# Another table of order and engines for the first two batches of an attention and feed-forward kernel

## The chip, the cores and the metric

The kernel runs on one core of a Trainium2 chip. The metric is device time in microseconds (us) of one launch; the kernel before takes 1108.86 us, the median of three runs (1108.12 to 1110.11). Five engines work side by side, each through its own queue in order: PE (TensorE, matmuls), DVE (VectorE), ACT (ScalarE), POOL (GpSimd) and SP (SyncE, which here only issues DMA transfers). They meet through semaphores.

## The reference

The reference is attention with a thresholded softmax over 8 batches of 8 heads, 576 positions of 64, followed by a feed-forward layer over the 4608 rows that come out of it:

```
scores = scale * q @ k.T
thresh = max(scores) - tau
scores = where(scores >= thresh, scores, -1e9)
attn   = exp(scores - max(scores)); attn /= sum(attn) + 1e-9
x      = (attn @ v), heads side by side            # 4608 x 512
h      = x @ w_in                                   # 512 x 2048
g      = h if h >= 1, 0 if h <= -1, else (h+1)^2/4
out    = g @ w_out                                  # 2048 x 512
```

## The kernel before

All matmuls but those of batch 0's scores run on f16 pairs: a value is split into a high half and a low rest, and each product is three matmuls (high by high, high by low, low by high). The weights arrive as 64-bit numbers, 16 blocks of 128x512 of `w_in` ("i") and 16 of `w_out` ("o"). Each goes through two steps before the feed-forward can use it. The first rebuilds a 32-bit number from the two words (`fix` L845, `low` L855, `b2` L864, `b3` L872); the letter in `SIGN` says how: "A" has ACT do both `fix` and `low`, "N" gives `low` to POOL, "D" gives `fix` to POOL and adds a second DVE instruction (`b3`). The second scales it and splits it into halves (L920 to L958); the letter in `CONV` says how: "A" and "G" are a scaling and a high half on ACT or on POOL and the rest on POOL (L933), "D" is the high half on POOL (L936) and the rest on DVE (L939), "P" and "Q" have PE form the rest and ACT (L949) or DVE (L947) copy it out. ACT's or POOL's results of the first step often need a PSUM bank `ph`, of which there are three.

Scores are computed in tiles of 128 rows by 576 columns, two tiles to a "visit" (`PAIR`: "J" runs the two together, "S" one after the other). A tile goes through a negated minimum on DVE (L1127), a threshold on DVE or ACT (`THR`: L1134 or L1132), the exponential on ACT (L1137), mask and sum on DVE (L1151), normalisation on POOL (L1169, the default) or on ACT (L1172, "N" in `TILE`), the high half on ACT (L1177), the rest on POOL (L1180), a transposing DMA (L1213), and the product with v on PE (L1299). Batch 0 is tiles 0 to 35. The feed-forward goes by groups of 256 rows; its matmuls all stand on line 466, its activation on L1376 to L1393.

The order of the instructions on every engine is not found by dependencies at run time: `Plan.op` numbers some 5000 steps, `ORDER` lists these numbers, and `Plan.order` (L329) walks the list, gives each step a time from its cost and its buffers, and the program is written out in order of these times. Buffers of a pool (PSUM banks `ph` and `s`, SBUF tiles) go to the step that takes them next in the list. Where PE would stand idle within the first 120 us of these times, `gaps` and `keep_warm` (L1451 to L1471) write small matmuls on constants into a free PSUM bank (L1454), which compute nothing that is used: 397 of them.

Of the kernel before, what the change touches and what calls it, by code (L numbers as in the profile page):

```python
# [26 lines left out]
CONV = {"i": "AGAGDAGGPAGAADDP", "o": "PDDAADMDAAPGAGAD"}  # L27

SIGN = {"i": "NNNAAANANANAANNA", "o": "AAAANANAAANANNNA"}
THR = "VVAVAVVVVVVVVVAVAAVVAAAAVVVVVAAVVVVAAVAAVAVVVAAVVVVVVAVVVVVVVVVVVVVVVVVVVVVVVVVVVVVVVVVVVVVVVVVVVVVVVVVVVVVVVVVVVVVVVVVVVVVVVVVVVVVVVVVVVVVVVVVVVVVVVVVVVVVVVVVVVVVVVVVVVVVVVVVVVVVVVVVVVVVVVVVVVVVVVVVVVVVVVVVVVVVVVVVVVVVVVVVVVVVVVVVVVVVVVVVVVVVVVVVVVVVVVVVVVVVVVVVVVVVVVVVVVVVVVVVVVVVVVVVV"  # L30
# [338 lines left out]
def attn_ffn_kernel(ctx: ExitStack, tc: tile.TileContext, qT, kT, vT, tau, w_in, w_out, out):  # L369
# [444 lines left out]
    def add_w(w):  # L814
# [96 lines left out]
        for u in range(NU):  # L911
# [48 lines left out]
            seen, done = [], []  # L960
            for how in plan.ways(("parts " + w, u), CONV[w][u], "PQAGDM"):
                if how in "AG":
# [548 lines left out]
```

## Time and profile before

| | before |
|---|---|
| median of three runs | 1108.86 us |
| the profiled execution | 1107.48 us |
| its span, first to last instruction | 1105.6 us |
| PE busy | 1080.7 us (98%) |
| DVE busy | 910.5 us (82%) |
| ACT busy | 876.5 us (79%) |
| POOL busy | 750.9 us (68%) |
| the L1454 matmuls' share of PE busy | 30.17 us |

The profile comes from one execution. Its own time is 1.38 us under the median of the runs, and 1.88 us of it lie outside the span. A busy share over the whole span says little here, since the first 170 us, where weights are converted beside attention, have other limits than the rest. So the rows below are read stretch by stretch. "Idle before <- X" in a row is idle time of the engine just before the instruction, and X is what released it.

### The profile page before, as it was taken

What the parts mean: (1) busy time and instruction counts of PE and PEld (TensorE: products, weight loads), DVE (VectorE), ACT (ScalarE), POOL (GpSimd) and SP (SyncE); (2) the same over time, 40 slices, a digit from 0 to 9 for tenths busy, and PEclk for the clock granted to TensorE, in tenths of its full rate; (3) what the DMA queues carried; (4) which work ended last, traced back from release to release, by engine and by line L of the source; (5) the groups of instructions that cost most, each with busy time, mean ns of one, the idle gap of its engine ahead of it and who ended that gap; (6) DMA issues with size and microseconds to landing.
All of it is one profiled execution on the core that took longest, in us unless ns stands there. A gap on an engine that the chain in (4) does not pass through costs nothing.

```text
span 1105.6 us, 36892 instructions
## 1 busy us (share of the span) xinstructions
PE 1080.7 (98%) x14677; PEld 800.8 (72%) x14677; DVE 910.5 (82%) x2664; ACT 876.5 (79%) x1682; POOL 750.9 (68%) x870
## 2 busy tenths in 40 slices
PE   8799989999999999999999999999999999999998
PEld 7578658777777777776777677677777677767774
DVE  4899988999889898889899898888888899877222
ACT  5899899898788898887788888778788886776433
POOL 4889997676668886797669786576667885565000
PEclk9699999999999999999999999999999999999999
DMA  9896798786877776798787777758667677558000
GB/s 337 294 272 129 144 205 160 120 147 120 171 135 147 160 137 135 132 156 148 126 148 149 128 151 139 128 114 165 148 114 119 120 123 141 95 97 137 12 20 20
DMA packets 420669, 155.90 MB, mean 141 GB/s; under 512 B 399504, under 2 KB 399504, under 8 KB 420496
## 3 DMA queue, kind: packets, MB, share of 16 engines
q1 hardware_dynamic: 420416, 153.41, 71.2%
q8 instruction: 115, 1.88, 0.7%
q14 instruction: 58, 0.48, 0.2%
q10 hardware_dynamic: 80, 0.13, 0.0%
HBM read 45.09 MB, written 9.44 MB: 49 GB/s over the span
## 4 chain that ended last, share of the span: by engine, by line
PE 80%; DVE 7%; ACT 5%; POOL 3%; issue 2%; DMA 2%; SPq 0%; ACTq 0%; DVEq 0%; POOLq 0%
PE ph L466 30%; PE acc L466 30%; PE s L1073 9%; PE ph L1299 9%; DVE s L1127 2%; DVE e L1151 2%; POOL hl L1180 1%; PE ph L1454 1%; DMA eT<-hl 1%; ACT e L1137 1%; ACT hl L1177 1%; POOL e L1169 1%; DMA x<-in_moe_w_out_dram 1%; DMA qq<-in_q_dram 0%; DVE sm L1134 0%
## 5 line engine op out<-in xcount | busy, mean ns | idle before, releaser
L466 PEld LDWEIGHTS <-WI 128*64 128x64 f16 (+1 forms) x7446 | 407.3, 108 | 53.3 <-issue 16.6
L1180 POOL TENSOR_TENSOR hl<-e,hl 128x576 f16<-128x576 f32 x267 | 347.8, 1311 | 118.0 <-ACT hl L1177 110.5
L466 PE MATMUL ph<-x,WI 128*64 128x256 f16 (+1 forms) x6912 | 400.3, 264 | 0.9 <-DVE x L1311 0.9
L1169 POOL TENSOR_SCALAR e<-e,sm 128x576 f32<-128x576 f32 x253 | 199.3, 792 | 111.9 <-DVE sm L1161 82.8
L1151 DVE SCALAR_TENSOR_TENSOR e<-s,sm,e 128x578 f32<-128x578 f32 x286 | 229.9, 813 | 21.8 <-ACT e L1137 16.4
L1137 ACT ACTIVATE e<-s,sm 128x576 f32<-128x576 f32 x288 | 209.0, 740 | 39.4 <-DVE s L1127 33.1
L1127 DVE TENSOR_SCALAR_CACHE_REDUCE s<-s,pc 128x576 f32<-128x576 f32 x252 | 203.6, 820 | 37.4 <-PE s L1073 36.0
L1177 ACT ACTIVATE hl<-e 128x576 f16<-128x576 f32 x267 | 178.6, 681 | 43.5 <-POOL e L1169 42.2
L466 PE MATMUL acc<-WO,ga 128*64 128x512 f16 (+1 forms) x1590 | 203.8, 380 | 0.2 <-ACT ob L1438 0.2
L1073 PE MATMUL s<-kk,qq 64*128 64x288 f16 (+3 forms) x1840 | 152.0, 299 | 9.1 <-DVE e L1151 8.1
L466 PEld LDWEIGHTS <-ga 128*64 128x64 f16 (+1 forms) x1590 | 91.9, 109 | 81.2 <-issue 9.8
L1383 DVE SCALAR_TENSOR_TENSOR ph<-ph,fcs,asq 128x512 f32<-128x512 f32 (+1 forms) x160 | 111.7, 700 | 45.2 <-ACT asq L1379 44.0
L1376 ACT ACTIVATE asq<-ph,fcs 128x512 f32<-128x512 f32 (+1 forms) x160 | 116.1, 735 | 37.9 <-PE ph L466 37.2
L1299 PE MATMUL ph<-eT,vst 128*64 128x320 f16 (+2 forms) x1928 | 123.8, 279 | 4.5 <-DMA eT<-hl 3.7
L1299 PEld LDWEIGHTS <-vst 128*64 128x64 f16 x1928 | 102.3, 110 | 23.1 <-issue 11.5
L1073 PEld LDWEIGHTS <-qq 64*128 64x128 f16 (+1 forms) x1680 | 66.3, 96 | 49.8 <-issue 37.4
L1388 ACT ACTIVATE ga<-ph,fcs 128x256 f16<-128x256 f32 (+1 forms) x160 | 70.3, 451 | 30.3 <-DVE ph L1383 23.7
L1379 ACT ACTIVATE asq<-asq 128x512 f32<-128x512 f32 x144 | 90.3, 629 | 3.2
L1393 DVE SCALAR_TENSOR_TENSOR ga<-ph,fcs,ga 128x256 f16<-128x256 f32 (+1 forms) x160 | 70.6, 449 | 24.2 <-ACT gb L1388 9.6
L466 PE MATMUL acc<-WO,gb 128*64 128x512 f16 (+1 forms) x582 | 75.0, 379 | 0.0
L466 PE MATMUL acc<-WO,WI 128*64 128x512 f16 (+1 forms) x534 | 68.3, 380 | 0.0
L466 PE MATMUL acc<-WO 128*64 128x512 f16 (+1 forms) x510 | 64.6, 380 | 0.0
(185 smaller groups left out, 1181.1 us busy)
## 6 DMA issues: line engine op xcount, KB each, us to landing
raw<-in_v_dram SPq DMA_DIRECT2D x32, 288.0 KB, 3.6
WO<-in_moe_w_in_dram SPq DMA_DIRECT2D x16, 512.0 KB, 7.3
out_dram<-ob SPq DMA_DIRECT2D x32, 256.0 KB, 2.8
raw<-in_q_dram SPq DMA_DIRECT2D x28, 288.0 KB, 3.4
raw<-in_k_dram SPq DMA_DIRECT2D x28, 288.0 KB, 3.2
x<-in_moe_w_out_dram SPq DMA_DIRECT2D x10, 512.0 KB, 5.9
eT<-hl SPq DMA_TRANSPOSE x288, 3.5
WO<-in_moe_w_out_dram SPq DMA_DIRECT2D x4, 512.0 KB, 5.0
```

Source lines behind the costliest of these rows:

```text
L466: T.matmul(out[x], lhsT[:, x], rhs, **flags)
L1073: T.matmul(ap(sb, s_ps)[r, f, :SH], q, k, start=ql == kl == 0, stop=exact or ql == 1)
L1127: V.tensor_scalar(sv(), sv(), c, None, ALU.mult, ALU.min, accum_out=t[:, 0:1])
L1137: A.activation(ev(), sv(), AF.Exp, bias=ap(m, sm)[:, 0:1], scale=-1.0)
L1151: V.scalar_tensor_tensor(ev(SH + 1), sv(SH + 1), t[:, 2:3], ev(SH + 1), ALU.is_le, ALU.mult, accum_out=t[:, 3:4])
L1169: G.tensor_scalar(ev(), ev(), ap(m, sm)[:, 5:6], ESC, ALU.mult, ALU.mult)
L1177: A.activation(part2(0), ev(), AF.Copy)
L1180: G.tensor_tensor(part2(w), ev(), part2(0), ALU.subtract)
L1299: T.matmul(o[hd * D : (hd + 1) * D, :n], vt[:, k, hd * D : (hd + 1) * D], t[:, kb, (hd ^ p % 2) * n : ((hd ^ p % 2) + 1) * n], start=m == ...
L1376: A.activation(tv()[:, :, c], hv()[:, :, c], AF.Relu, bias=fcs[:, b, 2, q : q + 1], scale=fcs[:, b, 3, q : q + 1])
L1379: A.activation(ap(tb, asq), ap(tb, asq), AF.Square)
L1383: V.scalar_tensor_tensor(hv()[:, :, c], hv()[:, :, c], fcs[:, b, 0, q : q + 1], tv()[:, :, c], ALU.max, ALU.min)
```

## The change

Only tables change: `CONV`, `SIGN`, `THR`, `PAIR`, `TILE` and `ORDER`. No function is touched.

```diff
-CONV = {"i": "AGAGDAGGPAGAADDP", "o": "PDDAADMDAAPGAGAD"}
+CONV = {"i": "AGAGGAGGPAGAADDP", "o": "PDDAADMGAAQGAGAD"}
-SIGN = {"i": "NNNAAANANANAANNA", "o": "AAAANANAAANANNNA"}
+SIGN = {"i": "NNNAADANAAANANAA", "o": "AAAANANAAANANNNN"}
-TILE = {3: "S", 5: "N", 7: "N", 8: "N", 18: "V", 20: "N", 25: "V", 26: "N", 27: "N", 28: "N", 29: "V", 32: "N", 35: "N", 40: "N", 44: "N", 54: "N", 55: "V", 58: "N", 59: "N", 69: "V",
+TILE = {3: "S", 5: "N", 8: "N", 18: "V", 20: "N", 22: "N", 25: "V", 26: "N", 27: "N", 29: "V", 30: "N", 32: "N", 55: "V", 69: "V",
...
 ORDER = [
-    605, 606, 607, 608, 12, 13, 14, 15, 0, 1, 590, 595, 596, 580, 585, 16, 17, 592, 600, 18, 597, 610, 5, 615, 19, 20, 21, 22, 591, 2, 598, 635, 581,
...
```

In words: block 4 of `w_in` and block 7 of `w_out` go from "D" to "G", block 10 of `w_out` from "P" to "Q". In `SIGN`, block 5 of `w_in` becomes "D", blocks 6, 8, 10 and 14 become "A", blocks 7 and 11 become "N", and block 15 of `w_out` becomes "N". In batch 0 the tiles 7, 28 and 35 leave the list of those that ACT normalises and 22 and 30 join it; in batch 1 the tiles 40, 44, 54, 58 and 59 leave it. Of the thresholds seven more go to ACT, four of them ahead of the first feed-forward product of the second group of rows. Of the visits 3, 5, 15 and 16 are joined, and 6, 7, 12 and 18 are parted. The keep-warm matmuls of L1454 fall from 397 to 314.

SP's queue near the start: `raw` are blocks of v, `WO` from `in_moe_w_in_dram` are staged blocks of w_in, `kk0` and `qq0` are k and q of the first heads. Before, from the tenth transfer on:

```order
L571 DMA kk0_76<-in_k_dram 128x576 [waits DMAHW3_49]
L839 DMA WO_68<-in_moe_w_in_dram 128x1024 [waits DMAHW4_49]
L513 DMA tcs_138<-in_tau_dram 128x1 [waits DMAHW5_49]
L839 DMA WO_68<-in_moe_w_in_dram 128x1024 [waits DMAHW6_49,DVE_49]
L571 DMA qq0_80<-in_q_dram 128x576 [waits DMAHW7_49]
L839 DMA WO_68<-in_moe_w_in_dram 128x1024 [waits DMAHW0_49,DVE_49,Activation_49]
```

And now, from the tenth on:

```order
L839 DMA WO_68<-in_moe_w_in_dram 128x1024 [waits DMAHW3_49]
L839 DMA WO_68<-in_moe_w_in_dram 128x1024 [waits DMAHW4_49]
L571 DMA kk0_76<-in_k_dram 128x576 [waits DMAHW5_49]
L571 DMA qq0_80<-in_q_dram 128x576 [waits DMAHW6_49]
L839 DMA WO_68<-in_moe_w_in_dram 128x1024 [waits DMAHW7_49,DVE_49]
L839 DMA WO_68<-in_moe_w_in_dram 128x1024 [waits DMAHW0_49,DVE_49]
```

The load of q is issued ahead of the block of w_in that waits for a DVE instruction, and no longer behind it.

ACT's queue at the exponentials of tiles 3 and 2 (into the buffers `e2` and `e3`; L862 is `low` of a weight block into a PSUM bank `ph`). Before:

```order
L1177 ACTIVATE hl0_93<-e1_90 128x576 [waits Pool_49]
L1137 ACTIVATE e2_91<-s1_62,sm2_124 128x2x288 [waits DVE_49]
L862 ACTIVATE ph1_64<-x4_107 128x512 [waits DMAHW4_49,PE_49]
L1137 ACTIVATE e3_92<-s0_61,sm3_125 128x2x288 [waits DVE_49]
L1132 ACTIVATE sm3_125<-sm3_125,tcs_138 128x1
L853 ACTIVATE x2_105<-x2_105 128x512 [waits DMAHW0_49]
```

And now:

```order
L1177 ACTIVATE hl0_93<-e1_90 128x576 [waits Pool_49]
L862 ACTIVATE ph0_63<-x4_107 128x512 [waits DMAHW5_49,DVE_49]
L1137 ACTIVATE e2_91<-s1_62,sm2_124 128x2x288 [waits DVE_49]
L1132 ACTIVATE sm3_125<-sm3_125,tcs_138 128x1 [waits DVE_49]
L1137 ACTIVATE e3_92<-s0_61,sm3_125 128x2x288
L862 ACTIVATE ph2_65<-x2_105 128x512 [waits DMAHW6_49,DVE_49]
```

The `low` that stood between the two exponentials and waited for PE stands ahead of both, in another bank, and waits for DVE and its load instead.

POOL's queue some rows on, at block 4 of w_in (`hl` are tiles' rests). Before, L936 is the high half of block 4, the L924 ahead of it scales block 6, the L930 and last L933 split block 6, and the first L933 is the rest of block 5:

```order
L924 TENSOR_SCALAR WI_67<-WI_67,wsc_i_141 128x512
L936 TENSOR_SCALAR WI_67<-WI_67,wsc_i_141 128x512
L933 TENSOR_TENSOR WI_67<-WI_67 128x512
L1180 TENSOR_TENSOR hl0_93<-e1_90,hl0_93 128x576
L1169 TENSOR_SCALAR e0_89<-e0_89,sm0_122 128x2x288
L860 TENSOR_SCALAR WO_68<-WO_68 128x512
L930 TENSOR_SCALAR WI_67<-WI_67 128x512
L933 TENSOR_TENSOR WI_67<-WI_67 128x512
```

And now, where the first L930 and L933 are those of block 4 (whose scaling stands a few rows ahead), and the second pair splits block 6:

```order
L860 TENSOR_SCALAR WO_68<-WO_68 128x512
L930 TENSOR_SCALAR WI_67<-WI_67 128x512
L933 TENSOR_TENSOR WI_67<-WI_67 128x512
L930 TENSOR_SCALAR WI_67<-WI_67 128x512
L933 TENSOR_TENSOR WI_67<-WI_67 128x512
L1180 TENSOR_TENSOR hl2_95<-e3_92,hl2_95 128x576
```

POOL has three instructions for block 4 where it had one.

## Rows read from the trace of the kernel before

**Rows 1.** Timeline of PE, the first 256-column product: start, us, engine, line.

```profile
168.91 5.41 PE L466 MATMUL ph<-x,WI 128*64 128x256 f16 x96
```

**Rows 2.** Windows: us; busy of PE, PEld, DVE, ACT, POOL; clock; DMA share; GB/s.

```profile
0.00:22.60 22.60, 19.81 (x232) 17.82 (x232) 7.54 (x24) 10.48 (x20) 8.27 (x46) 1.00 0.92 335
22.60:89.00 66.40, 56.18 (x632) 43.66 (x631) 60.55 (x178) 59.10 (x111) 56.83 (x70) 0.87 0.99 277
89.00:159.00 70.00, 66.45 (x791) 47.56 (x792) 66.49 (x193) 64.79 (x129) 67.17 (x74) 1.00 0.80 152
169.00:1000.00 831.00, 829.02 (x11743) 615.74 (x11739) 730.30 (x2154) 685.62 (x1309) 598.71 (x658) 1.00 0.75 136
```

**Rows 3.** The first three windows again, keep-warm matmuls of L1454 alone: PE busy.

```profile
0.00:22.60 22.60, 11.78 (x148) 1.00 0.92 335
22.60:89.00 66.40, 14.36 (x189) 0.87 0.99 277
...
sum 159.00, PE 30.17; mean PE 10.06
```

**Rows 4.** The chain of waits from 28 to 48 us: start, us, what.

```profile
31.78 3.92 PE ph L1454 x39
...
35.73 0.63 ACT ph L862
...
37.24 0.84 DVE e L1151 x2
...
42.48 1.27 POOL hl L1180
```

**Rows 5.** Timeline of ACT, one wait: start, us, engine, line [idle before <-releaser].

```profile
35.73 0.63 ACT L862 ACTIVATE ph<-x 128x512 uint32<-128x512 uint32 x1 [1.73 <-PE ph L1454]
```

**Rows 6.** The chain of waits from 88 to 105 us.

```profile
92.78 1.61 PE acc L1454 x27
94.40 1.18 PE s L1073 x7
```

**Rows 7.** Groups by line and form, 0 to 169 us: count | busy us, mean ns.

```profile
L1169 POOL TENSOR_SCALAR e<-e,sm 128x576 f32<-128x576 f32 x26 | 20.9, 807 | 3.4 <-DVE sm L1161 2.0 <-ACT WO L922 0.8 <-DVE sm L1203 0.4
L933 POOL TENSOR_TENSOR WI<-WI 128x512 f16<-128x512 f32 x11 | 12.7, 1161 | 0.3
L1172 ACT ACTIVATE e<-e,sm 128x576 f32<-128x576 f32 x9 | 7.0, 779 | 0.0
L870 DVE SCALAR_TENSOR_TENSOR WI<-WO,ph 128x512 uint32<-128x512 uint32 x8 | 5.3, 675 | 7.7 <-ACT ph L862 7.7
L1134 DVE TENSOR_SCALAR sm<-sm,tcs 128x1 f32<-128x1 f32 x25 | 5.3, 213 | 0.8
L1132 ACT ACTIVATE sm<-sm,tcs 128x1 f32<-128x1 f32 x15 | 4.2, 286 | 0.0
L924 POOL TENSOR_SCALAR WI<-WI,wsc_i 128x512 f32<-128x512 f32 x5 | 3.5, 695 | 5.2 <-DVE tcs L507 5.1
L939 DVE SCALAR_TENSOR_TENSOR WI<-WI,wsc_i 128x512 f16<-128x512 f32 x3 | 3.4, 1138 | 0.0
L930 POOL TENSOR_SCALAR WI<-WI 128x512 f16<-128x512 f32 x5 | 3.1, 617 | 0.7 <-PE ph L942 0.4
```

**Rows 8.** Timeline of DVE at the first attention tile.

```profile
24.96 0.68 DVE L868 SCALAR_TENSOR_TENSOR WI<-ph,WO 128x512 uint32<-128x512 uint32 x1
25.56 0.81 DVE L1127 TENSOR_SCALAR_CACHE_REDUCE s<-s,tcs 128x576 f32<-128x576 f32 x1
```

**Rows 9.** Who POOL waited for, 22.6 to 89 us: us, times, longest.

```profile
POOL hl L1180 <- ACT hl L1177: 4.8, 3, 2.3
```

**Rows 10.** One window of PE's low clock (columns of rows 2).

```profile
38.50:52.00 13.50, 11.07 (x55) 7.87 (x54) 11.12 (x31) 11.64 (x21) 10.76 (x14) 0.51 0.81 226
```

**Rows 11.** Timeline of PE, two like visits at different clocks.

```profile
24.24 2.09 PE L1073 MATMUL s<-kk,qq 64*128 64x288 f32 x8
...
46.47 3.98 PE L1073 MATMUL s<-kk,qq 64*128 64x288 f32 x8 [2.43 <-DVE e L1151]
```

More of the change, by code (lines that the diff above doesn't have):

```diff
@@ L25 @@
 XJ, XS = 1.2, 1.0
-CONV = {"i": "AGAGDAGGPAGAADDP", "o": "PDDAADMDAAPGAGAD"}
-SIGN = {"i": "NNNAAANANANAANNA", "o": "AAAANANAAANANNNA"}
-THR = "VVAVAVVVVVVVVVAVAAVVAAAAVVVVVAAVVVVAAVAAVAVVVAAVVVVVVAVVVVVVVVVVVVVVVVVVVVVVVVVVVVVVVVVVVVVVVVVVVVVVVVVVVVVVVVVVVVVVVVVVVVVVVVVVVVVVVVVVVVVVVVVVVVVVVVVVVVVVVVVVVVVVVVVVVVVVVVVVVVVVVVVVVVVVVVVVVVVVVVVVVVVVVVVVVVVVVVVVVVVVVVVVVVVVVVVVVVVVVVVVVVVVVVVVVVVVVVVVVVVVVVVVVVVVVVVVVVVVVVVVVVVVVVVV"
-PAIR = "SJSSSSJJJSSSJJJSSJJJJJJJJJJJJJJSJJJJJJJJJJJJJJJJJJJJJJJJJJJJJJJJJJJJJJJJJJJJJJJJJJJJJJJJJJJJJJJJJJJJJJJJJJJJJJJJJJJJJJJJJJJJJJJJJJJJJJJJJJJJJJJJ"
+CONV = {"i": "AGAGGAGGPAGAADDP", "o": "PDDAADMGAAQGAGAD"}
+SIGN = {"i": "NNNAADANAAANANAA", "o": "AAAANANAAANANNNN"}
+THR = "VVAVVVVVVVAAVVAAAAAAAAAAVAVVVVAVVVAAVVAAVVAAVVVVAAAAVVAVVVVVVVVVVVVVVVVVVVVVVVVVVVVVVVVVVVVVVVVVVVVVVVVVVVVVVVVVVVVVVVVVVVVVVVVVVVVVVVVVVVVVVVVVVVVVVVVVVVVVVVVVVVVVVVVVVVVVVVVVVVVVVVVVVVVVVVVVVVVVVVVVVVVVVVVVVVVVVVVVVVVVVVVVVVVVVVVVVVVVVVVVVVVVVVVVVVVVVVVVVVVVVVVVVVVVVVVVVVVVVVVVVVVVVVVV"
+PAIR = "SJSJSJSSJSSSSJJJJJSJJJJJJJJJJJJSJJJJJJJJJJJJJJJJJJJJJJJJJJJJJJJJJJJJJJJJJJJJJJJJJJJJJJJJJJJJJJJJJJJJJJJJJJJJJJJJJJJJJJJJJJJJJJJJJJJJJJJJJJJJJJJJ"
 QHOW = "DDPDPPDPPPDDPPPPPPPPPPPPPDDPPPPP"
@@ L248 @@
 NPLAIN = 4
-TILE = {3: "S", 5: "N", 7: "N", 8: "N", 18: "V", 20: "N", 25: "V", 26: "N", 27: "N", 28: "N", 29: "V", 32: "N", 35: "N", 40: "N", 44: "N", 54: "N", 55: "V", 58: "N", 59: "N", 69: "V", 71: "V", 94: "V", 114: "V", 117: "V", 150: "V", 152: "V", 173: "V", 181: "V", 186: "V", 200: "V", 214: "S", 222: "V", 257: "V", 262: "V", 287: "V"}
+TILE = {3: "S", 5: "N", 8: "N", 18: "V", 20: "N", 22: "N", 25: "V", 26: "N", 27: "N", 29: "V", 30: "N", 32: "N", 55: "V", 69: "V", 71: "V", 94: "V", 114: "V", 117: "V", 150: "V", 152: "V", 173: "V", 181: "V", 186: "V", 200: "V", 214: "S", 222: "V", 257: "V", 262: "V", 287: "V"}
 FSCALE = "GGGGGGGG"
```

401 rows, old and new, of the table ORDER are left out of this document.

## The prediction

> **What bounds the kernel now.** I read the page's busy shares first: PE is far ahead of the others (98%, DVE 82%). So I asked next where PE is not busy or busy for nothing, with a table of windows and the same table for the keep-warm matmuls alone. From 169 to 1000 us PE is busy 829.02 of 831 us [rows 2]: there it is the bound, and an engine that gets more or less to do changes nothing while it stays under its neighbours (POOL 72%, DVE 88%). Before that, PE loses time: to 22.6 us 2.8 idle and 11.78 keep-warm, from 22.6 to 89 us 10.2 idle and 14.36 keep-warm, from 89 to 159 us 3.55 idle and the remaining 4.03 keep-warm [rows 2, 3]. The first product over 256 columns, the second group's, starts at 168.91 [rows 1] and marks the change. What the tables can win or lose is won or lost in this lead. Its limit is the three elementwise engines together: from 22.6 to 89 us DVE, ACT and POOL are busy 91%, 89% and 86%, from 89 to 159 us 95%, 93% and 96% [rows 2]. None has much room; they pass the work round and wait a little for each other. The first 22.6 us are loading: DMA busy 0.92 at 335 GB/s [rows 2]. The change leaves PE's useful work as it is, so the time follows from when the lead ends.
>
> **The change part by part.** I make the sum against the profiled execution's own 1107.48 us (span 1105.6 and 1.88 outside it), and move it to the median of the runs, 1108.86, by the 1.38 us between them.
>
> *Term a, ACT's wait for a keep-warm block.* In the chain of waits from 28 to 48 us stands a block of 39 keep-warm matmuls, 3.92 us; when it ends, ACT starts a weight block's `low` in the same PSUM bank, behind it in ACT's queue comes an exponential, and DVE masks with that at 37.24 [rows 4]. ACT had been idle 1.73 us [rows 5]. In the new order that `low` is ahead of both exponentials and waits for no PE work, and the block of 39 is gone. What is late next: DVE, whose list just before the mask loses the rest of block 4 (1.138 us, [rows 7]), then PE's next scores, which waited for that mask. I take 1.73 as won. The ends are 0, if the POOL work that follows in the same chain up to 43.75 [rows 4] hides it, and 3.92, the whole block.
>
> *Term b, a shorter keep-warm block at 92.78.* There the chain goes from 27 keep-warm matmuls, 1.61 us, straight to scores [rows 6]. The block has 13 now: 14 x 1.61/27 = 0.83 us won. It is 0 if the scores' operands or their bank come only then, as the planned gap suggests, and can be no more than 1.61.
>
> *Term c, work that changes engines in the lead.* Counted ahead of the first feed-forward product of the second group of rows (168.91, [rows 1]). Two blocks go from "D" to "G": each gives POOL a scaling, a high half and a rest, 0.695 + 0.617 + 1.161, for one scaled high half, which I price like the scaling (0.695): 1.778 more, and takes 1.138 from DVE [rows 7]; two make 3.56 and -2.28. Tiles 7, 28 and 35 come to POOL and 22 and 30 go to ACT: one more normalisation on POOL, 0.807, one less on ACT, 0.779 [rows 7] (the scalar-sized divisors left out). Four more thresholds go to ACT: -4 x 0.213 = -0.85 on DVE, +4 x 0.286 = 1.14 on ACT [rows 7]. `SIGN` evens out on ACT and POOL by counts (one `low` for one `fix` on each) and gives DVE one `b3`; its nearest row is L870, 0.675 [rows 7]. Block 10 of w_out moves one copy out of PSUM from ACT to DVE; DVE has no row for it, and the rows of its shape lie between 0.617 and 1.161; I take L870, which also reads PSUM, for both engines [rows 7]. Sums: POOL +4.37, DVE -1.78, ACT -0.31, together +2.28. The three are about equally full, so if the order keeps them so, the lead grows by a third of it, 0.76 us. The ends are -1.78 (DVE alone is the bound) and +4.37 (POOL alone is). The five tiles of batch 1 that leave ACT come after 169 us: POOL gets 5 x 0.807 there, hidden under PE's 99.8%.
> VectorE's rest of a block has a mean of 1.138 us [rows 7]. The Trainium skill (SBUF — State Buffer, "SBUF: two separate sides") says that VectorE and GpSimd hold a shared port pair exclusively for a whole instruction, and that the other fully blocks; by that rule part of this price is waiting for GpSimd, which is given more to do here, so that DVE would get back less than the row says. By it the gain of 2.28 on DVE would be an upper bound, and the term somewhat above 0.76; no row here says how much.
>
> *Term d, the first tile.* The load of the first q stood behind a load of w_in that waits for DVE; now it goes ahead, with one block of w_in (512 KB, at 335 GB/s [rows 2] 1.56 us) less before it. DVE is in the way, though: its list up to the first tile's minimum at 25.56 is busy, and of it only the 0.68 us at 24.96 [rows 8] are moved behind the minimum. I take these 0.68 as won; the ends are 0 and 1.56. DVE does that work later all the same; the gain is that ACT's and POOL's first attention work comes sooner.
>
> *Elsewhere.* Of eight visits four are joined and four parted, all on PE; its 10.2 us of idle time from 22.6 to 89 us and 3.55 behind that [rows 2] hide what does not cancel. Were that cover gone, one visit more or less would be up to 2.09 us [rows 11].
>
> Sum: -1.73 - 0.83 + 0.76 - 0.68 = -2.48 us. From 1107.48 that is 1105.0, and from the median 1108.86 it is 1106.4.
>
> **The rivals.** *Fewer idle PE slots, all of it kept.* The order has 83 keep-warm matmuls fewer. In this trace 397 took 30.17 us of PE [rows 3], 0.076 each; 83 are 6.3 us. If useful work moves up into all of that, the time is 1108.86 - 6.3 = 1102.6. For it: from 169 us on every us that PE starts earlier is kept, since it idles 2 in 831. Against it: the blocks only fill gaps, and what PE waits for in the gaps are three engines at 86 to 96%.
>
> *POOL hides the gain.* After the mask at 37.24 the chain goes through POOL [rows 4]; if POOL, with block 4 added at just this place, is what comes last anyway, term a is 0 and the sum -0.75: 1108.1.
>
> *POOL becomes the bound of the lead, and the kernel is slower.* From 89 to 159 us POOL is busy 67.17 of 70 us, more than DVE (66.49) and ACT (64.79) [rows 2], and the last rests of batch 0 stand at the end of its list. The change puts 4.37 us on it. Before 89 us it has 9.6 us of idle time, but half of that (4.8 us, three waits for ACT's high half [rows 9]) comes from a tile's way from POOL to ACT and back, and work added ahead of such a trip moves the trip rather than fills it. Then the end of batch 0 comes 4.37 us later, the gains of a, b and d lie on engines that wait for POOL, and the time is 1113.2. The point from which it decides is the first stretch in which POOL's list has no wait, here 89 us. Against it: POOL would start earlier with tiles 0 to 3 (terms a and d).
>
> *PE's clock.* From 38.5 to 52 us PE runs at the lower of its two levels (0.51 granted, [rows 10]). A visit took 2.09 us at 2.4 GHz and 3.98 at 1.2 [rows 11]. What PE did before the fall was the block of 39 and a pause for the mask; the new order has no such block there. If one more visit falls into the low stretch, 1.89 us come back, and the sum is -0.59: 1108.3. The Trainium skill (TensorE: Matmul & The Clock Gate, "What's actually happening") has it that the default state is throttled and activity releases it; by that rule taking keep-warm work away speaks for this rival. The trace agrees in so far as the low window is the one with 2.4 us of PE idle among 13.5 [rows 10].
>
> **How the numbers follow.** I give the forecast 0.42, with its own range from 1104.0 to 1108.4 (each of a, b and d between half and one and a half of its value, c between 0 and 1.6); all of the keep-warm time kept 0.13, the gain hidden by POOL 0.17, POOL as bound 0.20, the clock 0.08. A measurement can tell about 0.2%, 2.2 us, from no change: faster means under 1106.6, slower over 1111.1. Faster: a little over half of the forecast, all of the first rival, a little of the second: 0.41. Slower: nearly all of POOL as bound and small parts of the rest, 0.25. Within: 0.34. The range for 8 in 10 goes from 1102.5, where the first rival ends, to 1112.0, within the POOL case, whose full 4.37 needs all its gaps to stay.
>
> **What would show it.** Term a: no wait of ACT for a keep-warm matmul between 30 and 45 us, and the mask of tile 2 about 2 us before 37.24. Term b: scores right behind 13 keep-warm matmuls with no idle PE. Term d: the first L1127 at about 24.9. Term c: in a window like 89 to 159 us, DVE under POOL by more than now. All together: the first 256-column product of L466, at 168.91 now, 2 to 3 us sooner, and behind it PE at 99.8% as before. I am wrong if that product starts sooner and the end does not, or if POOL shows no wait from some point before 89 us on and that product is late: then POOL was the bound. A low clock well beyond 52 us would speak for the clock.

## The result: 11 us faster, and the profile after

| | median of the runs, us | its runs | ratio to before |
|---|---|---|---|
| before | 1109.03 | 1108.12 to 1110.11 (4) | |
| after | 1098.07 | 1096.96 to 1099.07 (4) | 0.990, 95% interval 0.9887 to 0.9912 |

The forecast was 1106.4, with 1102.5 as the lower end: the direction was right, the size was off by more than a factor of four (2.5 us against 11.0). The profiled execution of after took 1099.07 us (span 1097.3), the slowest of its four runs, and that of before 1107.48, under the fastest of its own, so the two traces differ by only 8.4 us. The other 2.6 of the 11 us are the distance of these two executions from their medians, and no trace shows where they lie.

The 256-column product, in PE's timeline of after (columns as in [rows 1]):

```profile
161.60 0.61 PE L466 MATMUL ph<-x,WI 128*64 128x256 f16 x8
```

It starts 7.31 us earlier than 168.91 [rows 1]. The windows of after (columns as in [rows 2]):

```profile
0.00:22.60 22.60, 19.80 (x237) 17.66 (x238) 9.69 (x29) 10.52 (x20) 9.77 (x49) 1.00 0.93 341
22.60:89.00 66.40, 55.19 (x654) 42.57 (x655) 60.98 (x187) 63.52 (x123) 63.56 (x78) 0.90 1.06 288
89.00:159.00 70.00, 66.45 (x730) 43.79 (x730) 65.84 (x189) 63.88 (x130) 66.96 (x75) 1.00 0.89 161
162.00:1000.00 838.00, 835.77 (x11845) 619.35 (x11843) 734.53 (x2163) 687.62 (x1316) 610.86 (x672) 1.00 0.75 137
```

Behind the product PE is busy 99.7%, 99.8% before [rows 2]; from the product to the end of the span it is 935.7 us now and 936.7 before. So of the 8.3 us by which the traced spans differ, 7.31 lie in the lead. From 22.6 to 89 us ACT is busy 63.52 us (59.10 before) and POOL 63.56 (56.83), in the same 66.4 us. The keep-warm matmuls of L1454 in the first three windows of after (busy of PE and PEld; clock; DMA share; GB/s):

```profile
0.00:22.60 22.60, 12.20 (x158) 10.83 (x158) 1.00 0.93 341
22.60:89.00 66.40, 9.69 (x131) 8.47 (x131) 0.90 1.06 288
89.00:159.00 70.00, 1.92 (x25) 1.40 (x25) 1.00 0.89 161
```

The lead can be accounted for exactly: its length is the sum of what DVE, ACT and POOL are busy and idle in it, divided by three. This is bookkeeping, which holds for any stretch; it says where the time went and not why. Here is the window from 22.6 us to the product, first of before, then of after:

```profile
22.60:168.91 146.31, 130.72 (x1514) 96.12 (x1514) 134.08 (x393) 131.29 (x256) 132.64 (x155) 0.94 0.89 211
```

```profile
22.60:161.60 139.00, 124.24 (x1422) 88.14 (x1424) 129.09 (x382) 130.00 (x259) 132.95 (x156) 0.95 0.96 219
```

With the first 22.6 us added [rows 2], the three engines work 424.30 us in the lead before (134.08 + 131.29 + 132.64 + 26.29) and 422.02 after, 2.28 less; they are idle 82.43 us before (3 x 168.91 - 424.30) and 62.78 after, 19.65 less. (-2.28 - 19.65) / 3 is the 7.31. So nine tenths of the gain in the lead are idle time, spread over three engines. Of the 19.65 us, 3.69 lie ahead of 22.6 us and can't be put down to the change: there the three engines' work is 27.2 to 29.0 us in five other executions that begin with before's order (k1, k2, m1, s2 and s3 below; 26.29 in before) and 27.6 to 30.9 in ten that begin with after's (29.98 in after). From 22.6 to 89 us they are idle 22.7 us in before (3 x 66.4 less what they are busy [rows 2]) and 11.1 in after. That is found in other executions too: 23.6 in s3, which has before's order up to there, and 9.9, 11.8 and 9.9 in p3, c5 and v1, which have after's. The window of s3:

```profile
22.60:89.00 66.40, 54.76 (x640) 42.55 (x638) 60.01 (x178) 58.53 (x111) 57.09 (x71) 0.90 1.02 277
```

Who waited from 22.6 to 89 us: the longest waits of ACT before (us in all, times, longest),

```profile
ACT e L1137 <- DVE s L1127: 1.9, 3, 1.1
ACT ph L853 <- PE ph L789: 1.8, 1, 1.8
ACT ph L862 <- PE ph L1454: 1.7, 1, 1.7
ACT vst L765 <- PE s L760: 1.6, 1, 1.6
```

ACT's after,

```profile
ACT junk L685 <- DMA raw<-in_v_dram: 1.4, 1, 1.4
ACT vst L765 <- PE s L760: 1.3, 1, 1.3
ACT WI L922 <- DVE wsc_i L794: 1.0, 1, 1.0
```

and POOL's after, beside [rows 9]:

```profile
POOL WI L933 <- ACT WI L928: 0.2, 1, 0.2
POOL hl L1180 <- ACT hl L1177: 0.2, 1, 0.2
```

In this stretch ACT no longer waits for a PSUM bank, and POOL's 4.8 us for ACT's high halves have become 0.2. Single waits differ between executions of one order, though: in s3 ACT's wait for the bank of L789 (1.8 here) isn't there, and POOL's 4.8 are 2.9. Where in the lead the gain was won is seen from a progress curve: the time by which the three engines together have done so much work since 0 us (from windows of 5 us, interpolated; one execution each, and kernels with the same first part differ by up to 2.4 us here, so smaller differences say little; the four below after are explained further on).

| work done, us | 50 | 100 | 150 | 200 | 300 | 440 |
|---|---|---|---|---|---|---|
| before | 31.2 | 51.1 | 69.7 | 88.0 | 123.4 | 175.2 |
| after | 29.5 | 47.0 | 64.7 | 82.9 | 117.2 | 168.1 |
| p1_head | 29.7 | 48.5 | 68.7 | 89.9 | 125.0 | 177.2 |
| p2_to_av0 | 30.2 | 47.6 | 66.1 | 86.4 | 121.6 | 172.9 |
| p3_to_first_group | 29.8 | 47.2 | 64.5 | 82.3 | 119.0 | 170.4 |
| s3_after_late | 30.2 | 48.7 | 67.7 | 87.3 | 121.8 | 172.6 |

After is 1.7 us ahead of before at 30 us, 4.1 at 50, 5.0 at 70, between 5 and 6.2 from there to 120 us, 7.1 at the end. The execution of before is a late one at the start, though. The first 50 us of work are done at 30.1 to 30.7 us in the five others with its order, and at 29.2 to 30.6 in those with after's, so nothing is shown to be won by 30 us. The first 100 are done at 48.7 us in s3 and 50.4 in s2, which has before's order up to 60 us, so 1.7 to 4.1 us are won by there.

### The profile page after: what moved, and what is told of

It is laid out like the page before. It is cut to its first block, busy times and chain, and to the rows that moved or that the text cites. A ratio compares the mean times of both kernels' runs of the same rounds, so it can differ in the third digit from the quotient of the medians.

```text
span 1097.3 us, 36713 instructions
## 1 busy us (share of the span) xinstructions
PE 1073.0 (98%) x14591; PEld 790.6 (72%) x14591; DVE 906.1 (83%) x2651; ACT 871.2 (79%) x1682; POOL 759.4 (69%) x880
## 4 chain that ended last, share of the span: by engine, by line
PE 80%; DVE 10%; DMA 5%; POOL 2%; issue 2%; ACT 1%; SPq 0%; DVEq 0%; POOLq 0%; ACTq 0%
PE acc L466 30%; PE ph L466 30%; PE s L1073 9%; PE ph L1299 9%; DMA eT<-hl 2%; DVE s L1127 2%; DVE e L1151 2%; POOL hl L1180 1%; PE ph L1454 1%; DMA qq<-in_q_dram 1%; DMA kk<-in_k_dram 1%; DMA raw<-in_v_dram 1%; DVE ph L1383 1%; POOL e L1169 0%; DVE WO L939 0%
## 5 line engine op out<-in xcount | busy, mean ns | idle before, releaser
L1180 POOL TENSOR_TENSOR hl<-e,hl 128x576 f16<-128x576 f32 x267 | 347.3, 1309 | 107.7 <-ACT hl L1177 101.8
L1169 POOL TENSOR_SCALAR e<-e,sm 128x576 f32<-128x576 f32 x259 | 203.5, 790 | 106.6 <-DVE sm L1161 75.3
L466 PEld LDWEIGHTS <-ga 128*64 128x64 f16 (+1 forms) x1590 | 91.2, 109 | 82.3 <-issue 9.9
L1388 ACT ACTIVATE ga<-ph,fcs 128x256 f16<-128x256 f32 (+1 forms) x160 | 70.2, 450 | 29.2 <-DVE ph L1383 22.4
L466 PE MATMUL acc<-WO,gb 128*64 128x512 f16 (+1 forms) x546 | 71.0, 379 | 0.0
L466 PE MATMUL acc<-WO 128*64 128x512 f16 (+1 forms) x546 | 69.4, 380 | 0.0
```

What stands on the lines that cost most here:

```text
L466: T.matmul(out[x], lhsT[:, x], rhs, **flags)
L1169: G.tensor_scalar(ev(), ev(), ap(m, sm)[:, 5:6], ESC, ALU.mult, ALU.mult)
L1180: G.tensor_tensor(part2(w), ev(), part2(0), ALU.subtract)
```

## The experiments

Theories: **W**, single waits of ACT and POOL hold up what stands behind them; **H**, the earlier start; **B**, the ways (which engine does what); **O**, order and ways as a whole. Times of before are those of the same set of runs, and a ratio is not just that of the two medians. A product is that of one execution and so as loose as the curve above. The keep-warm blocks are placed anew from the plan in each kernel.

**Keep-warm blocks left out.** Three edits to the one line that places them:

```diff
-        left = gaps(order)
+        left = [x for x in gaps(order) if int(x[2] / WARM[3]) != 39]     # k1, in before
+        left = [x for x in gaps(order) if x[0] < 20.0]                   # k2 in before, k5 in after
```

> The kernel before with one thing less: the block of 39 keep-warm matmuls (31.8 to 35.7 us in its trace) isn't written. Theory A (ACT's wait for a PSUM bank that keep-warm work or PE's queue holds starts a delay that all three elementwise engines then share): ACT's wait of 1.73 us at 35.7 goes, the first feed-forward product starts 2 to 4 us sooner than 77.5, and the time falls by 1.7 to 4 us, to about 1105 to 1107. Theory B (the gain of the change comes from which engine does what: fewer of the slow rests on DVE): no more than 1 us. Theory C (it comes from the order as a whole): no more than 1 us.

> The kernel before without any keep-warm matmul from about 22 us on (after the first eight blocks); nothing else changes. Theory A: ACT loses the wait of 1.73 us and part of the one of 1.77 us, the time falls by 2 to 5 us. The rival of the clock: PE stays at 1.2 GHz for much longer than the 17 us before, and the time grows by 2 us or more. Theories B and C: within 1 us of before.

> The changed kernel without any keep-warm matmul from about 22 us on (after the first nine blocks). Theory A: no ACT wait hangs on these blocks any more, so the time stays within 1 us of the changed kernel's 1098. The rival of the clock: slower by 2 us or more, since PE's clock stays low through the first feed-forward products.

| | median, us | ratio [95%] | 256-column product |
|---|---|---|---|
| before | 1108.36 | | 168.91 |
| k1_no39 | 1106.24 | 0.9982 [0.9969, 0.9994] | 168.54 |
| k2_before_nowarm | 1104.50 | 0.9971 [0.9960, 0.9982] | 167.05 |
| k5_after_nowarm | 1100.02 | 0.9935 [0.9910, 0.9961] | 164.64 |

Without the block of 39 the wait of 1.73 us is gone, and the wait for the next bank has grown from 1.8 to 3.0. ACT's longest wait of k1 from 22.6 to 89 us:

```profile
ACT ph L853 <- PE ph L789: 3.0, 1, 3.0
```

k1 is 2.1 us faster, as theory A has it (in these first expectations A is W, and C is O), but not in the way that it says: the first feed-forward product comes at 78.77 us, 1.3 later than the 77.48 of before and not 2 to 4 sooner. Without any keep-warm block behind 20 us both waits are gone, and 0.3% is won in before (k2). In after the same edit (k5) seems to lose 0.35%, with intervals that just touch: its product comes 3.0 us later, in the slowest of its four executions, with PE's granted clock at 0.77 from 22.6 to 89 us instead of 0.90. The clock alone doesn't explain that, since k2, which wins, has 0.77 there too, and before 0.87. So the blocks cost before something, by k2 about three tenths of the gain, and seem to be worth something to after.

**The two waiting instructions moved.** ACT's queue in before. With the moves the plan asks for 63 keep-warm matmuls ahead of the first; they are held at 28:

```diff
-L862 ACTIVATE ph_64<-x_107 128x512
 L1137 ACTIVATE e_92<-s_61,sm_125 128x2x288
 L1132 ACTIVATE sm_125<-sm_125,tcs 128x1
+L862 ACTIVATE ph_64<-x_107 128x512
...
-L853 ACTIVATE ph_63<-WO 128x512
 L1137 ACTIVATE e_91<-s_61,sm_126 128x2x288
 L1132 ACTIVATE sm_127<-sm_127,tcs 128x1
 L1137 ACTIVATE e_90<-s_62,sm_127 128x2x288
+L853 ACTIVATE ph_63<-WO 128x512
```

> Before, with two ACT instructions moved in ACT's queue alone: the low that waited 1.73 us at 35.73 behind the next exponential and threshold, and the fix into a bank that waited 1.77 us at 44.07 behind the two exponentials that followed it. The keep-warm block in the bank of the first is held at 28 matmuls. Theory W (an instruction that waits holds up what stands behind it on its engine, and these two waits of ACT are a third to a half of what is lost from 31 to 70 us): first feed-forward product 2 to 3.5 us earlier than 77.48, 256-column product at 166 to 167.3, time 1105 to 1106.5. Rival (what stands behind them meets the next wait): first feed-forward product within 1 of 77.5, 256-column product within 0.6 of 168.9, time 1107.5 to 1109.

Measured 1109.47 against 1109.08, ratio 1.0012 [0.9998, 1.0027], product at 169.49: the rival's, and W's 1105 to 1106.5 is excluded. ACT's timeline in before and in m1 (columns as in [rows 5]):

```profile
36.29 0.72 ACT L1137 ACTIVATE e<-s,sm 128x576 f32<-128x576 f32 x1
```

```profile
33.82 0.74 ACT L1137 ACTIVATE e<-s,sm 128x576 f32<-128x576 f32 x1 [0.36 <-DVE s L1127]
...
44.53 1.17 ACT L853 ACTIVATE ph<-WO 128x512 f32<-128x512 f32 x2 [1.67 <-PE ph L1454]
```

The exponential that came at 36.29 in before comes at 33.82. Of these 2.5 us, 0.9 are m1's earlier start (first minimum at 24.69, 25.56 in before [rows 8]), so about 1.6 are won there. At 44.53 ACT waits 1.67 us for another keep-warm block. The first feed-forward product comes at 80.59, later than in before, and the gain is gone: removed waits of before are replaced.

**Half an order.** Three kernels follow after's order up to a step and before's from there on, and three have other halves. Ways (`CONV`, `SIGN`, `THR`, `PAIR`, `TILE`) go with the order that a block or tile begins in. For p2, without the lines of `TILE`, `THR`, `PAIR` and `ORDER`:

```diff
-CONV = {"i": "AGAGDAGGPAGAADDP", "o": "PDDAADMDAAPGAGAD"}
+CONV = {"i": "AGAGGAGGPAGAADDP", "o": "PDDAADMDAAPGAGAD"}
-SIGN = {"i": "NNNAAANANANAANNA", "o": "AAAANANAAANANNNA"}
+SIGN = {"i": "NNNAADANAAANANAA", "o": "AAAANANAAANANNNA"}
...
```

> The order of after up to its 126th step (about the first exponential of attention, 25 us, with the loads, the first weight blocks and the first scale), then the order of before; SIGN of the w_in blocks 5, 6 and 10 as in after (the blocks begun in that part), the rest of the tables as before. The block of 39 keep-warm matmuls and the low that waits for it stay as in before. Theory H (the gain begins with an earlier start: first minimum 25.56 to 23.74, first scale of w_in 22.33 to 21.37, and an earlier start is carried to the end because the three engines are full behind it): first minimum near 23.8, first 256-column product near 167.1 (before 168.91), time about 1106.5. Theory W (the gain lies in waits of ACT and POOL between 28 and 70 us): the start is earlier, the next wait is longer by as much, product within 0.5 of 168.9, time 1108 to 1109. Theory O (an order is worth something only whole): new waits at the seam, product at 169 to 174, time 1109 to 1114.

> The order of after up to its second product with v (about 55 us), then that of before; blocks and tiles begun in that part with the ways of after (block 4 of w_in G, SIGN of w_in as after, tile 7 not normalised by ACT), everything later as before. ACT has no wait for a keep-warm block in it. Theory W: the waits removed before 55 us carry: second product with v near 56 (before 62.00), 256-column product at 163 to 165, time 1103 to 1105. Theory H alone: product near 167, time 1107. Theory O: product at 169 or later, time 1109 or more.

> The order of after up to its 460th step (all blocks rebuilt, the first group of the feed-forward begun, about 80 us), then that of before; what stays as in before is the second step of w_out (CONV of o), the tiles 22, 28, 30 and 35 and the thresholds and visits of later tiles. Theory W: first feed-forward product near 69.8 (before 77.48), 256-column product at 162 to 164, time 1099.5 to 1102: nearly all of the gain, and the changes behind it worth 2 us at most. Theory B (the ways, DVE's fewer slow rests, of which block 7 of w_out is missing here): product near 164.5, time 1102 to 1104. Theory O: 167 or later, 1106 or more.

> The reverse of the third part-order: before up to its 455th step (about 85 us), then the order of after, with the ways of after for blocks, tiles, thresholds and visits begun there. If the late part is worth what the whole has beyond the early part (11.0 less 6.0 to 6.6), and the parts add up: product at 164.5 to 166, time 1104 to 1105. If the late part of after is worth nothing without its early part: product at 168 to 169.5, time 1108 to 1109.5. Theory O: 1110 or more.

> Before up to its 292nd step (about 60 us), then the order and ways of after. If the parts add up: 11.0 less the 4.5 to 5 that after's order up to 55 us gave, so 6 us under before: product near 164, time 1102 to 1103.5. If the early waits decide and later parts only pass them on: within 1.5 us of before. Theory O: 1110 or more.

| | after's order | median (before), us | ratio [95%] | product |
|---|---|---|---|---|
| p1_head | to 25 us | 1109.56 (1108.33) | 1.0005 [0.9993, 1.0018] | 171.36 |
| p2_to_av0 | to 55 us | 1103.30 (1108.33) | 0.9959 [0.9946, 0.9971] | 166.61 |
| p3_to_first_group | to 80 us | 1101.76 (1108.33) | 0.9946 [0.9925, 0.9967] | 163.65 |
| after | whole | 1098.07 (1109.03) | 0.9900 [0.9887, 0.9912] | 161.60 |
| s3_after_late | from 85 us | 1108.04 (1109.08) | 0.9993 [0.9981, 1.0004] | 166.30 |
| s2_after_from_av0 | from 60 us | 1106.36 (1109.08) | 0.9977 [0.9962, 0.9991] | 169.99 |

The early start doesn't carry the gain (H falls): p1 has its first minimum at 23.96 us, before had 25.56 [rows 8], and by the interval p1 is at most 0.8 us faster than before. Its time and product are those of theory O (the profiled execution, 1111.33 us, is its slowest). Its engines wait longer. POOL's longest wait in p1, and DVE's, from 22.6 to 89 us:

```profile
POOL WI L930 <- PE ph L942: 3.8, 1, 3.8
```

```profile
DVE s L1127 <- PE s L1073: 3.5, 2, 2.5
```

By the ratios the stretch from 25 to 55 us gives 0.46% (p1 to p2), that from 55 to 80 us 0.13%, which is inside the noise, and what lies behind 80 us again 0.46% (p3 to after). So none of them can be called the largest. Each such kernel also has a seam with waits of its own (p1's above, one in p2 below), so that a difference is one of two whole kernels and not the price of a stretch. p2 and p3 have the times that W forecast for them, but W also had 2 us at most behind 80 us, and there are 4 to 5. The late part alone (s3) can't be told from before; after's order from 60 us on (s2) gives 0.23%, which none of its three theories had. The parts don't add up: p3 and s3 together give 0.6%, p2 and s2 0.64%, the whole 1.0%.

**One wait of 3.34 us taken out of p2.** A block of 45 keep-warm matmuls had formed where the two orders meet. The edit is that of k1, with 45.

> The order of after up to its second product with v, then that of before, as in the second run of the last set, but without the block of 45 keep-warm matmuls that stood at 64.46 us for 3.50 us and for whose bank ACT waited 3.34 us; PE stands idle there instead. Theory W (a wait of ACT for a keep-warm block is paid in full at the end of the lead): product at 163.3 to 164 (with the block 166.61), time 3 us less than with the block, about 1100.5. Rival, another wait comes last (as where the block of 39 was left out of before: 1.2 of 1.73 us came back in the next wait): product 165.3 to 166.6, time within 1 us of 1103.3. Rival clock: PE's clock falls to the lower level behind 64 us and the product is later than 166.6.

Measured 1104.10 (before 1108.85), ratio 0.9959 [0.9944, 0.9974], the same as p2, so W's 3 us are excluded and the time is the rival's. The product comes at 164.73, between the two ranges and 1.9 earlier than in p2, whose profiled execution (1105.48 us) is its slowest; the runs don't show that gain. The wait as it stood in p2 (in p2b the same instruction starts at 64.50 without a wait), in ACT's timeline:

```profile
67.99 0.64 ACT L862 ACTIVATE ph<-WO 128x512 uint32<-128x512 uint32 x1 [3.34 <-PE ph L1454]
```

**Orders with the other's ways.** Only the tables are exchanged, f1 all five in after's order, f2 all five in before's, th2 only `THR` and `TILE`, c2 only `CONV`, c5 of `CONV` only block 4 of `w_in`, all in after's order:

```diff
-CONV = {"i": "AGAGGAGGPAGAADDP", "o": "PDDAADMGAAQGAGAD"}
+CONV = {"i": "AGAGDAGGPAGAADDP", "o": "PDDAADMDAAPGAGAD"}     # c2
+CONV = {"i": "AGAGDAGGPAGAADDP", "o": "PDDAADMGAAQGAGAD"}     # c5
```

> The order of the changed kernel with the old tables of engines and ways (CONV, SIGN, THR, PAIR, TILE as before); a step that exists only in the old ways stands where its like stands in the new order, and where a buffer isn't free a step goes behind the next that can go. The keep-warm blocks are written anew from the plan. Theory C (order): at least 5 of the 11 us are there, time 1103 or less. Theory B (ways): at most 3 of the 11 us, time 1106 or more. Theory A: what counts is whether ACT waits for PE's banks between 25 and 50 us; if it doesn't, about 1103.

> The order of before with all the other tables of after (CONV, SIGN, THR, PAIR, TILE); the counterpart of the run with after's order and before's tables, which was 28 us slower than before. Theory B (the ways carry the gain): faster than before, 1100 to 1106. Theory O (an order fits only the ways it was made for): 1115 to 1140, the elementwise engines well under 60 us busy of the 66.4 from 22.6 to 89. Prediction's term c alone: 1109 to 1110.

> After, with the tables THR and TILE as in before (so tiles 7, 28 and 35 and five of batch 1 are normalised by ACT, 22 and 30 by POOL, and four thresholds of the lead go back to DVE), the order kept. By the prediction's term c: -0.8 on POOL, +0.8 -1.14 on ACT, +0.85 on DVE, together -0.3, nothing in the time: product within 0.5 of 161.6, time 1097.5 to 1099. Theory B (these ways carry the part of the gain that lies behind 80 us): product 164 or later, time 1101 or more.

> After in everything, but CONV as in before: block 4 of w_in and block 7 of w_out formed by POOL's high half and DVE's rest again, block 10 of w_out copied out by ACT. By the prediction's term c (the sum of the three engines' work divided by three) this takes 3.56 us from POOL and gives DVE 2.28: 0.4 us faster, product near 161.2, time near 1098. By theory B (DVE is the engine that has no room, and each rest by DVE holds up what POOL does) 2.3 us or more slower: product near 164, time 1100.5 to 1103. Theory O: 5 us or more slower.

> After, with block 4 of w_in alone as in before (POOL's high half and DVE's rest, "D" for "G"), the order kept: POOL has 1.78 us less to do, DVE 1.14 more. By the prediction's term c: 0.2 us faster, product near 161.4. By theory B (the new way of w_in's early blocks carries the gain): 3 us or more slower, product 164 to 166. By the theory of waits: within 1 us of after, since in the last run with this way no engine waited at that place.

| | median (before), us | ratio [95%] | product |
|---|---|---|---|
| f1_order_new_ways_old | 1136.37 (1108.36) | 1.0264 [1.0238, 1.0289] | 180.43 |
| f2_order_old_ways_new | 1124.76 (1108.85) | 1.0141 [1.0119, 1.0164] | 179.14 |
| th2_after_thr_tile_old | 1128.45 (1109.08) | 1.0172 [1.0149, 1.0195] | 174.88 |
| c2_after_conv_old | 1103.66 (1108.33) | 0.9960 [0.9948, 0.9972] | 166.29 |
| c5_after_i4_D | 1098.39 (1108.85) | 0.9908 [0.9892, 0.9924] | 161.01 |

Exchanged whole, neither the ways (f2) nor the order (f1) brings the gain: each is slower than before. That doesn't show that the gain needs the new ways, since the old ones stand in an order that was made for others; the next run puts this right for `CONV`, and for `SIGN`, `THR`, `PAIR` and `TILE` it was not tried. th2 changes 0.3 us of work in the lead by the prediction's prices and is 30 us slower than after. Not all of that lies in the lead: its product comes 13.3 us later than in after, and from there to the end of the span (1126.3) it is 951.4 us, 935.7 in after. In f1 this rest is 950.0 us and in f2 943.6, so in these three the product doesn't stand for the end. What ACT and POOL waited for in th2 from 60 to 200 us, the longest:

```profile
ACT hl L1177 <- POOL e L1169: 11.1, 3, 5.4
ACT sm L1132 <- DVE s L1127: 6.5, 2, 4.1
```

```profile
POOL hl L1180 <- ACT hl L1177: 15.6, 11, 4.2
```

An engine that is given a step stands here in its place in the queue until the other has delivered, and the other then waits for it. c5 shows that the new way of block 4 costs and gives nothing that can be told. c2 seems to show that the rest of `CONV` is worth 5 us; the next run shows that it isn't.

**One instruction moved.** In c2 DVE waits for POOL's high half of block 7 of `w_out`. DVE's timeline there:

```profile
107.97 1.78 DVE L939 SCALAR_TENSOR_TENSOR WO<-WO,wsc_o 128x512 f16<-128x512 f32 x1 [2.52 <-POOL WO L936]
109.67 0.80 DVE L1210 SCALAR_TENSOR_TENSOR hl<-e,sm,hl 128x576 f16<-128x576 f32 x1
```

In c4 this rest stands 39 places later in `ORDER`, which is two dozen instructions of DVE's queue (the expectation says some ten); all else is as in c2.

> As the run before with CONV of before in the order of after, with one instruction moved: DVE's rest of block 7 of w_out, for which DVE had stood idle 2.5 us at 107.97 behind POOL's high half, stands some ten instructions later in DVE's queue, behind the sum of tile 24. The work is that of CONV of before. Theory of work (DVE's rests cost what they take, and DVE has no room): nothing changes, product near 166, time 1103 to 1104.5. Theory of waits (the loss was the one wait of DVE for POOL, and what queued behind it on ACT and POOL): product near 162, time 1098 to 1100, within 1 us of after, as the prediction's price of the two blocks (0.4 us in favour of the old CONV) allows.

Measured 1098.32 (before 1108.85), ratio 0.9911 [0.9891, 0.9930], product at 161.41. DVE's timeline in c4:

```profile
105.16 1.29 DVE L1210 SCALAR_TENSOR_TENSOR hl<-e,sm,hl 128x576 f16<-128x576 f32 x1
...
114.98 0.73 DVE L939 SCALAR_TENSOR_TENSOR WO<-WO,wsc_o 128x512 f16<-128x512 f32 x1
```

The same list of work, one instruction moved in one queue, 5 us, as the theory of waits has it: L1210 starts 4.5 us earlier, and the product 4.9. At the place itself 2.52 us of wait go and the 1.78 that the rest took there; where it stands now it takes 0.73. So a wait of 2.52 us put into an order that fits costs, with the longer instruction behind it, all of it and more, and the change of `CONV` by itself is worth nothing that can be told.

**A wait taken out of after.** One ACT instruction (L685, the wait of 1.4 us above) moved behind the exponential of tile 14:

```diff
-L685 ACTIVATE junk,vssq<-raw_69 128x576
 L853 ACTIVATE ph_64<-x_105 128x512
 L1376 ACTIVATE asq_100<-ph_63,fcs 128x512
...
 L1137 ACTIVATE e_91<-s_61,sm_124 128x2x288
+L685 ACTIVATE junk,vssq<-raw_69 128x576
```

> After, with one ACT instruction moved: the sum of squares of a block of v (L685), for which ACT stood idle 1.40 us at 75.25 until the load had come, stands four instructions of ACT later, behind the exponential of tile 14. All else as in after. It asks whether the order of after can be bettered by the same kind of move by which one order position was worth 5 us in the two runs with the old CONV. Theory of waits, in proportion to those runs (2.5 us of wait, 4.7 us of product): up to 2.6 us: 256-column product at 159 to 161, time 1095.5 to 1097.5. Rival, the next wait takes it (as in before with its two moved instructions): product within 0.6 of 161.6, time 1097.5 to 1099.

Measured 1097.27 (before 1108.33), ratio 0.9902 [0.9885, 0.9920], product at 161.08: no different from after. The time lies in W's range and the product in the rival's, so the run doesn't decide between them. None of c4, c5 and v1 can be told from after, so no version here beats it.

## Why the prediction was wrong

**The step that failed is what the sum put at nothing.** That the time follows from when the lead ends held for this change (7.31 of the 8.3 us between the traces). But of the idle time of the three elementwise engines, which it named as the lead's limit, the sum priced two waits of one chain (a and b) and the earlier start (d). The rest it put at nothing, with the sentence "None has much room; they pass the work round and wait a little for each other". The idle time of DVE, ACT and POOL was taken as a given; it was what the change changed. In the two traces it fell by 19.65 us in sum, 6.55 us of the lead, and the sum had 3.24 for that (a, b and d). Leaving out the 3.69 us ahead of 22.6 us, which are scatter, it is 15.96 and 5.32, and 11.6 of the 15.96 fell between 22.6 and 89 us, where the other executions agree.

**Term a (-1.73)**: right at its place, and open as a price. ACT's wait is gone, and the mask of tile 2 starts at 34.36, 2.88 earlier than 37.24 [rows 4]; against s2 and s3, which have before's order there (36.39 and 36.24), it is 1.9 to 2.0 earlier, and 2 were forecast. DVE's and ACT's timelines of after:

```profile
34.36 0.82 DVE L1151 SCALAR_TENSOR_TENSOR e<-s,sm,e 128x578 f32<-128x578 f32 x1
```

```profile
33.08 0.73 ACT L1137 ACTIVATE e<-s,sm 128x576 f32<-128x576 f32 x1
```

But moving this and the next waiting instruction alone gave nothing (m1), and leaving the block out gave 2.1 us (k1; 0.7 to 3.4 by its interval), which its trace doesn't show in the lead. What is late next was named as DVE and PE's scores; it was the next bank of ACT, held by L789 in k1 and by another keep-warm block in m1.

**Term b (-0.83)**: as forecast at its place, scores right behind 13 keep-warm matmuls, but nothing at the next product. PE in after:

```profile
87.76 0.90 PE L1454 MATMUL acc<-ones 128*128 128x128 bf16 x13
88.59 1.98 PE L1073 MATMUL s<-kk,qq 64*128 64x288 f32 x8
90.50 0.24 PE L1299 MATMUL ph<-eT,vst 128*64 128x128 f16 x1
91.16 1.00 PE L1299 MATMUL ph<-eT,vst 128*64 128x128 f16 x29 [0.42 <-DMA eT<-hl]
```

The scores come 5.8 us earlier than 94.40 [rows 6]; the feed-forward product ahead of them came 5.0 earlier, the next one 4.7 (96.82 before, 92.09 now). From the product ahead to the scores PE is 0.8 us quicker; then it waits 0.42 for a transpose and its scores take 0.6 longer than in before, so the 0.8 is not kept.

**Term c (+0.76)**: the sign was wrong and the term didn't matter. The work of the three engines fell by 2.28 us where it was to rise by 2.28: POOL's rose by 1.81 (4.37 priced), DVE's fell by 2.84 (1.78) and ACT's by 1.25 (0.31). The counts are as said (on POOL two more of L924, L930 and L933 each, two fewer of L936, one more of L1169); the durations are not, since one more L1169 costs 0.1 us in sum and 33 rests of tiles (L1180) take 43.9 us where they took 44.8. DVE's rests fell as said in count, from eight to six in the lead, 9.4 to 7.5 us. The rows that carry DVE's and POOL's share, of after from 0 to the product (columns as in [rows 7]):

```profile
L939 DVE SCALAR_TENSOR_TENSOR WO<-WO,wsc_o 128x512 f16<-128x512 f32 x4 | 5.9, 1463 | 0.1
L939 DVE SCALAR_TENSOR_TENSOR WI<-WI,wsc_i 128x512 f16<-128x512 f32 x2 | 1.6, 804 | 0.0
L1134 DVE TENSOR_SCALAR sm<-sm,tcs 128x1 f32<-128x1 f32 x21 | 4.4, 212 | 0.6
L933 POOL TENSOR_TENSOR WI<-WI 128x512 f16<-128x512 f32 x12 | 13.9, 1164 | 0.6 <-ACT WI L928 0.2
L1169 POOL TENSOR_SCALAR e<-e,sm 128x576 f32<-128x576 f32 x27 | 21.0, 783 | 0.2 <-DVE sm L1161 0.2
```

Two rests fewer gave back 1.9 us and not 2.28, since those that are left took longer (1.25 us in the mean, 1.18 before). Some of the fall is the same instruction in less time (L733, four times each: 5.0 us before, 3.9 now). That work can't be what decides is shown by c2 against c4 (the same list of work, 5 us apart), c5 and c4 (-0.2 and -0.4 priced, no change measured) and th2 (-0.3 priced, 30 us slower). Its sign came true all the same: from 89 to 159 us DVE is 1.12 us under POOL, 0.68 before [rows 2].

**Term d (-0.68)**: right in its place and nearly in its size. Between these two traces the first minimum moved by 1.82, but before's execution is a late one: in the five others with its order (k1, k2, m1, s2, s3) it comes at 24.46 to 25.12, so that 24.9 was no sign of the change. What the order changes is the distance from the first scale of `w_in` (L474) to the minimum: 3.79 or 3.80 us in all six, 2.92 to 2.94 in the eleven kernels with after's order there, so 0.85 us. L474 itself comes at no other time: 20.66 to 21.77 in the six, 20.48 to 21.80 in the eleven. DVE in before, then in after, then the minimum in s2:

```profile
21.77 0.16 DVE L474 TENSOR_SCALAR wsc_i<-ph 128x1 f32<-128x1 f32 x1 [0.72 <-PE ph L789]
```

```profile
20.80 0.16 DVE L474 TENSOR_SCALAR wsc_i<-ph 128x1 f32<-128x1 f32 x1 [0.75 <-PE ph L789]
23.74 0.82 DVE L1127 TENSOR_SCALAR_CACHE_REDUCE s<-s,tcs 128x576 f32<-128x576 f32 x1
```

```profile
24.74 0.80 DVE L1127 TENSOR_SCALAR_CACHE_REDUCE s<-s,tcs 128x576 f32<-128x576 f32 x1
```

As a gain it isn't seen by itself: p1 has it and is at most 0.8 us faster.

**The rivals.** "All keep-warm time kept" forecast 6.3 us less and was closest in size, but by the wrong mechanism: leaving out all the blocks behind 20 us gives 0.3% in before and nothing in after. "POOL hides the gain" (1108.1) and "POOL becomes the bound" (1113.2) both fail on POOL's idle time. The second is refuted at its decisive step, that work put ahead of a trip to ACT moves the trip rather than fills it: POOL's idle time from 22.6 to 89 us fell from 9.6 us (9.3 in s3) to 2.8, with 6.7 us more work done in it, and the trips' waits from 4.8 (2.9 in s3) to 0.2. "PE's clock" did not decide: the low level is still there (0.50 from 36 to 39 us, 0.51 from 45 to 51), with the gain made across it. The upper end that the forecast gives its own range, 1108.4, doesn't follow from the bounds that it names, which add up to 1108.8; nothing hangs on it.

What is shown, then: the gain in the lead is idle time of the three engines that is gone, not work that is gone; the early start alone doesn't bring it, and the change of `CONV` isn't needed for it; the kernels with half an order put it in about equal parts between 25 and 55 us and behind 80 us. What stays open is which waits of before matter: three tries to take one out (k1, m1, p2b) moved it to the next place or gave back only part of it, so no single one is shown as the cause of the gain. It isn't shown either whether the other tables are needed in an order made for the old ones, or why the late part is worth 0.46% only behind the early one.

## What to carry to other kernels

Where several in-order queues that feed each other are each about 90% busy, the time is work plus waits over the number of queues: take the idle time of all of them from the trace and ask how much of it a new order could remove, instead of adding up the waits of one chain and the work moved. That sum is an upper bound (here 82 us of idle time, of which 41.5 lie in the first 22.6 us of loading and 40.9, or 13.6 us of the lead, behind them), and it belongs into the forecast's range when an order is new as a whole. And judge a change of engine only with the order made for it: one instruction that waits in the wrong place cost 5 us here and hid that the change itself was worth nothing that could be told. Last, look at a second execution of an order before its trace is read for such sizes: here that takes away half of what the first one shows for the early start.

## What was not expected of the hardware

The same rest on DVE, 128x512, took 0.73 to 1.78 us, the long ones beside work of POOL where this was looked at. In before, DVE's at 35.36 and POOL's beside it:

```profile
35.36 1.55 DVE L939 SCALAR_TENSOR_TENSOR WI<-WI,wsc_i 128x512 f16<-128x512 f32 x1
```

```profile
35.08 1.28 POOL L1180 TENSOR_TENSOR hl<-e,hl 128x576 f16<-128x576 f32 x1
36.33 1.19 POOL L1169 TENSOR_SCALAR e<-e,sm 128x576 f32<-128x576 f32 x1
```

POOL's L1180 has its usual 1.28, DVE's rest takes twice the 0.75 it took in c4 at 38.52, where POOL was idle, and POOL's next, 0.75 elsewhere, takes 1.19: they look as if they had gone one after the other. The Trainium skill (SBUF — State Buffer, "SBUF: two separate sides") says that a VectorE and a GpSimd instruction that want the shared ports exclude each other for a whole instruction. The traces agree in these durations; no run here isolates it.

The other is how loose a trace is in the lead: kernels with the same order up to 80 us (before and s3) stood 2.4 us apart at 50 us in their profiled executions, the first minimum of before's order came at 24.46 to 25.56 us in six, and before's runs go from 1104.2 to 1111.8 us. A single trace can't place a gain of 2 us there.
